# Sparse attention and a gated convolution FFN on one core: the middle batches convolved over a whole batch in one token order, query mask rows rewritten per slot, DMA planned as one first-in-first-out server

## The chip, the core and the metric

The kernel runs on one core of a Trainium2 chip. The core has five engines with an instruction stream each, taken in order: PE (TensorE, matrix products into PSUM), DVE (VectorE), ACT (ScalarE), POOL (GpSimd) and SP (SyncE, which here only issues DMA). They wait for each other through semaphores. Sixteen DMA engines move data between DRAM and the on-chip SBUF, and between places in SBUF. The metric is device time in microseconds, from the start to the end of the program.

## What is computed

```python
scores = scale * np.matmul(q, k.transpose(0, 1, 3, 2))          # 4 batches, 8 heads, 768 tokens, 64 wide
mask = (|blk_i - blk_j| <= 1) | first and last block rows and columns | 3 sampled blocks per block row
attn = softmax(np.where(mask, scores, -1e9));  x = attn @ v     # heads side by side: 768 x 512 per batch
h = np.maximum(x @ w_in, 0.0)                                   # 512 -> 1024
conv_out[t] = conv_w[0] * h[t-1] + conv_w[1] * h[t] + conv_w[2] * h[t+1]   # zeros outside the batch
gate = 1.0 / (1.0 + np.exp(-conv_out))
out = (h * gate) @ w_out                                        # 1024 -> 512
```

A block has 32 tokens, so a batch has 24. The convolution runs along the tokens and couples neighbours, so the two halves of a batch meet at a seam.

## The kernel before

*Units.* The work is cut into 8 halves (a half is 384 query tokens of one batch, `n = 2b + g`) and each half into 18 units of eight 128x128 score blocks. A unit is a set of score products on PE into one `st` buffer (line 678), one exponential of 128x1024 on ACT (line 685), and eight products with V on PE into `av` (line 705). Four pairs of heads per half take 4.5 units each. After a pair DVE takes the reciprocal of the row sums and normalises (`rcp`, `xtok`, lines 629 and 631). SP then transposes `xtok` into `xT` by DMA (line 652); the first half and the last pair go through PE instead (line 644).

*Mask.* The mask is no separate step. Q and K lie in slots with 64 rows of a head and 24 rows more (64 to 88) that hold the block mask: an indicator of the key's block on K's side, and 8000-fold penalties on Q's side. One product of 88 rows gives score plus mask. There are six slots, for the pairs P = 0 to 15 in turn, each as an ET and an OT tile (even and odd token phase). The mask rows of slot 0 are made in the start (lines 413 to 455), those of slot 1 are copied by DVE and POOL, and those of slots 2 to 5 by DMA on SP's queue (lines 444 to 463). They are the same for all pairs, since q has the same token order in every batch.

*Token order.* K is loaded with six consecutive tokens per row. Q is loaded by `src_of` (line 342) half by half: within half g, row p holds the three tokens 384g + 3p + c. The score, `xT`, `hE` and `gT` tiles of a half so have 3 column groups c of 128 rows p. A shift by one token is a shift by 128 columns, except for the outer groups, where it goes to the neighbouring row.

*Loads.* POOL issues the DMA loads that cast to 16 bits (`swdge`, line 490): q, k and v per pair, and the weights. For P = 1 to 5 (`NPE = 6`) PE transposes q and k (line 533) and DVE copies them into the slots (line 539). Later pairs go through two DMA transposes on SP (line 581) and two DVE copies from `tmp` (line 424).

*FFN.* `ffn1` (line 719) makes 8 groups of 128 channels per half: four products each into `mix` (line 729), then a scaled ReLU into `hE` by DVE (742) or ACT (740). For each pair of groups POOL copies the edge columns (`edges`, lines 829 to 835), and `conv_gate` (line 746) runs three taps of two multiplications of 384 columns each on DVE (753), two sums (759), a tanh on ACT (769), an add of one (772) and the gate (781) into `gT`. At the seam the last column of half g = 0 lacks its right neighbour; POOL saves it in `cvl` (844), and three small DVE steps and one ACT step mend it (859 to 867). `out_block` (line 784) makes three blocks of 128 tokens per half, eight products each (799), an eviction to `o2s` (422 or 424) and a store.

*Order.* Nothing of this order is in the loops. Every step is entered as an operation with a planned duration, its dependencies, buffers and a due time, and `Scheduler.run` (line 205) lists them: `forward` takes the earliest start on each engine, `backward` turns the finished plan into priorities, and this is repeated. DMA is planned as engine "DQ", with a fixed latency behind each transfer:

```python
LAT = {"PE": 0.23, "ACT": 0.20, "DVE": 0.16, "POOL": 0.20, "SP": 0.0, "DQ": 1.9}
T0, PACE0, PACE1 = 8.0, 0.91, 1
XLAT, TLAT = 3.908, 9.2201
first_u = [18 * (2 * (P // 4)) + (P % 4) * 4.5 for P in range(NP)]
load_u = [0, 0, 0, 0, 15, 19, 24, 30, 42, 50, 60, 68, 77, 86, 96, 104]
```

The plan fixes the order on every engine and, for evictions, the engine itself. The chip then runs these streams with real waits. `helpers` such as `copy_to` (lines 420 to 424) stand in the profile with one line for several tiles.

Of the kernel before, what the change touches and what calls it, by code (L numbers as in the profile page):

```python
# [24 lines left out]
class Op:  # L25
    __slots__ = ("alts", "fn", "deps", "prio", "lat", "allocs", "earliest", "pend", "outs", "ready",
                 "start", "end", "eng", "key", "uses")

    def __init__(self, alts, fn, prio, deps, lat, earliest):
        self.alts, self.fn, self.prio = alts, fn, prio  # L30
        self.deps = deps
        self.lat = lat
        self.allocs, self.uses = [], []
        self.earliest = earliest
        self.outs = []
        self.start = self.end = self.eng = None
# [12 lines left out]
FLEX = 0.0345  # L49
LAT = {"PE": 0.23, "ACT": 0.20, "DVE": 0.16, "POOL": 0.20, "SP": 0.0, "DQ": 1.9}  # L50
OWN = {"PE": 0.0, "ACT": 0.12, "DVE": 0.11, "POOL": 0.10, "SP": 0.0, "DQ": 0.0}


class Scheduler:
# [22 lines left out]
    def forward(self):  # L77
# [11 lines left out]
        while left:  # L89
# [27 lines left out]
            for e, t in free.items():  # L117
                be = None
                for o in cand:
# [5 lines left out]
                    k = (s, o.prio, o.key)  # L125
                    if be is None or k < be[0]:
                        be = (k, o, e)
                if be is not None:
                    k2 = (be[0][0], be[0][1], be[0][2], be[0][0] + be[1].alts[e])
                    if best is None or (k2[0], k2[3]) < (best[0][0], best[0][3]):  # L130
                        best = (k2, be[1], e)
            if best is None:
                raise RuntimeError("no order: buffers too few")
            k, o, e = best
            o.eng = e
            o.start = k[0]
            o.end = k[0] + o.alts[e]
# [25 lines left out]
    def backward(self, order):  # L163
# [25 lines left out]
        while ready:  # L189
# [4 lines left out]
            for j in pred[i]:  # L194
                pend[j] -= 1
                if not pend[j]:
                    ready[j] = max(0.0, max(end[m] + lat for m, lat in succ[j]))
        for o, t in zip(order, end):
            o.prio = -t
            o.outs = []  # L200
            for b in o.allocs:
                b.index = None
                b.pool.holders = []
# [10 lines left out]
def kernel(  # L214
# [11 lines left out]
    nc = tc.nc  # L226
# [10 lines left out]
    NPE = 6  # L237
    NWARM = 34

# [19 lines left out]
    NTMP, NVN, NNAT, NPT, NXK, NXT, NHE, NCV, NGT, NOS = 2, 3, 3, 5, 3, 4, 3, 3, 4, 4  # L259
# [7 lines left out]
    hE_t = many(NHE, [128, NFFC, 640], BF16, "hE")  # L267
    m_t = many(NCV, [128, 2, 768], BF16, "m")
    tn_t = many(NCV, [128, 768], BF16, "tn")
    gT_t = many(NGT, [128, NFFC, 384], BF16, "gT")  # L270
# [11 lines left out]
    bblkn = sb.tile([NB, 6, 128], BF16, tag="bblkn", name="bblkn")  # L282
# [36 lines left out]
    T0, PACE0, PACE1 = 8.0, 0.91, 1  # L319
    OFF = 32.0894  # L320
    XLAT, TLAT = 3.908, 9.2201
    S_FIRST, A_FIRST, R_FIRST, N_FIRST = 5.6663, -4, 0.1178, 0.842
    F1S, F2A, F2S = 0.03, 2.344, 0.191
    WO = 22.9467
    OFFL = 28
    PE_ = 0.0
    PASSES = 12
# [10 lines left out]

    def dma_h(dst, src):
        return lambda e: (nc.sync if e == "SP" else nc.scalar).dma_start(out=dst, in_=src() if callable(src) else src)  # L340

    def src_of(t, b, h):

        if t is q:
# [7 lines left out]
    def dst_of(t, tile_, pair):  # L352
        if t is not q:
            return tile_
        return tile_.rearrange("p h (g c) -> p (h g) c", g=2) if pair else tile_.rearrange("p (g c) -> p g c", g=2)

    hw = {}
    for x, (t, h) in enumerate([(q, 0), (k, 0), (q, 1), (k, 1)]):
        i_ = op({"SP": 0.46} if x % 2 == 0 else {"ACT": 0.42}, dma_h(dst_of(t, stage0[x], False), src_of(t, 0, h)),
                [-20, -20, -18, -19][x], lat=0.4)  # L360
        hw[x] = dq([0.9, 0.4, 0.9, 0.4][x], [i_], [-20, -19, -17, -18][x])
# [17 lines left out]
    def ind(base, sign, src):  # L379
        return lambda e: nc.gpsimd.affine_select(  # L380
            out=bblkn, in_=src, compare_op=ALU.is_ge, fill=0.0, base=base,
            pattern=[[384 * sign, 2], [sign, 3], [3 * sign, 128]], channel_multiplier=-32 * sign)
# [30 lines left out]
    def w24(e):  # L413
        w = st_t[b_w.index]
        nc.tensor.matmul(out=w[0:NB, 0:384], lhsT=aadd, rhs=bblkn[:, 0:6:2, :], start=True, stop=True)
        nc.tensor.matmul(out=w[0:NB, 512:896], lhsT=aadd, rhs=bblkn[:, 1:6:2, :], start=True, stop=True)
# [9 lines left out]

    def k_rows(t, cs, b0):

        def fn(e):
            for (u, c0, n, at) in cs:  # L430
                src = bblkn.rearrange("k (g c) (j u) -> k u c g j", g=2, u=2)[:, u, c0:c0 + 2 * n - 1:2]
                dst = t[64:88, 1, 0, at:at + n].rearrange("k c (g j) -> k c g j", g=2)
                copy_to(e, dst, src)
        return fn
    km_e = op({"ACT": 0.6, "DVE": 0.4}, k_rows(ET[0], [(0, 0, 2, 0), (1, 1, 1, 2)], 0), -15, [bn2])
    km_o = op({"ACT": 0.6, "DVE": 0.4}, k_rows(OT[0], [(0, 1, 1, 0), (1, 0, 2, 1)], 0), -14.9, [bn2])

# [6 lines left out]
    def rows_to(dst, src):  # L444
        return lambda e: nc.sync.dma_start(out=dst[64:88], in_=src[64:88])

    def dup(t):
        return lambda e: copy_to(e, t[64:88, :, 1], t[64:88, :, 0])

# [4 lines left out]
    e_mask = {0: op({"POOL": 1.0}, pool_copy(ET[0][64:88, :, 1], ET[0][64:88, :, 0]), 1.5, [qm_e, km_e])}  # L454
    o_mask = {0: op({"DVE": 0.38}, dup(OT[0]), T(1), [qm_o, km_o], earliest=T0 - 0.5)}
    for s in range(1, NSLOT):
        for t, m in ((ET, e_mask), (OT, o_mask)):
            if s == 1 and t is OT:
                m[s] = op({"POOL": 1.8}, pool_copy(t[s][64:88], t[0][64:88]), 2.5, [m[0]])
            elif s == 1:  # L460
                m[s] = op({"DVE": 0.58}, rows_by(t[s], t[0]), T(4.5 * s) - 2.5, [m[0]])
            else:
                m[s] = op({"SP": 0.46}, rows_to(t[s], t[0]), T(4.5 * s) - 6, [m[0]], lat=6.0,
                          earliest=T(18 + 2 * s) if s > 3 else 0.0)
# [4 lines left out]
    for s in range(NHE):  # L469
        def z(e, s=s):  # L470
            nc.vector.memset(hE_t[s][:, :, 639:640], 0.0)
# [14 lines left out]
    load_u = [0, 0, 0, 0, 15, 19, 24, 30, 42, 50, 60, 68, 77, 86, 96, 104]  # L486
# [3 lines left out]
    def swdge(dst, src, prio, dur, deps=(), early=0.0, alloc=None, uses=(), gate=i_sel,  # L490
              lat=None):
        i_ = op({"POOL": 0.8}, lambda e: nc.gpsimd.dma_start(out=dst(), in_=src), prio,  # L492
                list(deps) + [gate], lat=0.0, alloc=alloc, uses=uses, earliest=early)
        return i_, op({"DQ": dur}, None, prio, [i_], lat=lat or 2.4, uses=(([alloc] if alloc else []) + list(uses)))

    win_ld, wout_ld, k_iss, v_iss = [], [], {}, {}
    def qk_loads(P):
        b, h0 = P // 4, 2 * (P % 4)
        nb = Buf(P_nat)
        early, late = (T(load_u[P]), 6.0) if P > 3 else (0.0, None)  # L500
        iq, lq = swdge(lambda: dst_of(q, nat_t[nb.index][:, 0], True), src_of(q, b, slice(h0, h0 + 2)), P, 1.25,
                       early=early, alloc=nb, gate=bn1 if P == 1 else i_sel, lat=late)
        if P == 1:
            bn2.deps.append(iq)
        ik, lk = swdge(lambda: nat_t[nb.index][:, 1], src_of(k, b, slice(h0, h0 + 2)), P + 0.1 if P > 1 else 0.6, 1.1, [iq],
                   early=early + (3 if P > 3 else 0), uses=[nb], lat=late)
# [3 lines left out]
    def v_load(P, deps):  # L510
# [3 lines left out]
        v_iss[P], ld = swdge(lambda: vn_t[vb.index], src_of(v, b, slice(h0, h0 + 2)), P + 1.15 if P < 3 else P + 0.2, 1.1,  # L514
                              early=T(load_u[P]) + 6 if P > 3 else 0.0, alloc=vb, lat=6.0 if P > 3 else None,
                              gate=k_iss[max(P, min(P + 1, 3))])

# [3 lines left out]
        return op({"DVE": 0.27}, cp, T(first_u[P]) - (1 if P == 0 else 6), [ld] + deps, uses=[vb, slot_b[P]])  # L521

# [405 lines left out]
```

The softmax here doesn't subtract the row's maximum and nothing guards it: scores larger than these inputs give would overflow.

## Time and profile before

| what | value |
|---|---|
| time, median of five runs | 214.82 us (214.74 to 216.77) |
| profiled execution | 214.87 us, its span 213.2 us |
| granted TensorE clock | 1.00 |
| first, 18th and last exponential | 8.2, 27.2 and 182.8 us (end for the last two) |
| DVE convolution: taps, sums, adds of one, gates | 57.0, 34.9, 11.6, 17.9 us busy |
| ACT: exponentials, tanh | 141.8, 27.7 us busy |
| moved by DMA | 25.84 MB, 121 GB/s on average |

A "busy" time counts an instruction from its start to its end, and neighbours overlap: the next one starts before the last has ended. The sum of durations is therefore more than the time taken, and the distance between starts is the better price of one more instruction. Idle time in a row of the page is what an engine waited just before its instructions, with the releaser that came last.

### The profile page before, as it was taken

To read this page: it belongs to the slowest core of one execution; us is meant where nothing else is said; L and a number is where in the kernel's file an instruction comes from. 1 tells how busy PE (TensorE), PEld (TensorE's weight loads), DVE (VectorE), ACT (ScalarE), POOL (GpSimd) and SP (SyncE) were. 2 spreads that over 40 slices of the span, in tenths; PEclk is the share of its full clock that TensorE was granted. 3 is DMA by queue.
4 is the path that set the end of the run, shared out by engine and by line. 5 is a ranking of instruction groups with operands and counts; after the bars stand their busy time and mean duration, and the time that the engine had idled before them with its cause. 6 is when DMAs were issued, how large, how long until landed. Compare 5 with 4: busy or idle time off the path is not lost.

```text
span 213.2 us, 6588 instructions
## 1 busy us (share of the span) xinstructions
PE 198.0 (93%) x2579; PEld 150.1 (70%) x2596; DVE 190.1 (89%) x541; ACT 182.2 (85%) x227; POOL 81.2 (38%) x174
## 2 busy tenths in 40 slices
PE   7898999997999979999989979989999999998992
PEld 4687879885778857788767657767776787554441
DVE  6977439999999998399999999999999999999972
ACT  4598999999989989999979799989999999664541
POOL 8996206335524720365557201421241012343300
PEclk9999999999999999999999999999999999999999
DMA  6999997999999994999997993002100220122223
GB/s 167 149 194 205 200 202 111 120 148 151 193 119 210 145 129 71 156 149 200 171 138 115 141 189 98 18 22 68 52 23 22 92 95 22 33 84 101 100 98 148
DMA packets 50519, 25.84 MB, mean 121 GB/s; under 512 B 36320, under 2 KB 47352, under 8 KB 50488
## 3 DMA queue, kind: packets, MB, share of 16 engines
q0 software_dynamic: 18464, 11.14, 45.7%
q1 hardware_dynamic: 31592, 13.75, 32.6%
q10 hardware_dynamic: 432, 0.52, 0.8%
q8 instruction: 20, 0.33, 0.6%
q14 instruction: 11, 0.09, 0.2%
HBM read 23.08 MB, written 6.29 MB: 138 GB/s over the span
## 4 chain that ended last, share of the span: by engine, by line
DVE 50%; PE 25%; DMA 8%; ACT 7%; issue 5%; POOL 4%; ACTq 0%; POOLq 0%; DVEq 0%
DVE m L753 18%; PE st L678 9%; DVE m L759 9%; DVE hE L742 6%; ACT pt L685 6%; PE mix L799 5%; PE av L705 4%; PE mix L729 4%; DVE gT L781 4%; DVE xtok L631 4%; DMA nat<-in_k_dram 3%; DMA xT<-xtok 3%; DVE tn L772 2%; PE st L799 2%; DVE o2s L424 2%
## 5 line engine op out<-in xcount | busy, mean ns | idle before, releaser
L685 ACT ACTIVATE pt<-st 128x1024 bf16<-128x1024 f32 x144 | 141.8, 1039 | 6.9 <-PE st L678 5.5
L705 PE MATMUL av<-vt,pt 128*128 128x65 bf16 x1152 | 57.9, 193 | 0.5 <-ACT pt L685 0.2
L753 DVE TENSOR_SCALAR m<-hE,cw 128x384 bf16<-128x384 bf16 x192 | 57.0, 346 | 0.2
L705 PEld LDWEIGHTS <-pt 128*128 128x128 bf16 x1152 | 50.4, 97 | 4.8 <-ACT pt L685 0.7
L729 PE MATMUL mix<-xT,winb 128*128 128x384 bf16 x240 | 48.3, 325 | 2.6 <-DMA xT<-xtok 1.2
L829 POOL COPY hE<-hE 128x254 bf16<-128x254 bf16 x32 | 18.2, 570 | 75.5 <-DVE hE L742 51.0
L799 PE MATMUL mix<-woutb,gT 128*128 128x512 bf16 x151 | 41.0, 379 | 2.4 <-DVE gT L781 1.6
L678 PE MATMUL st<-ot 88*128 88x128 bf16 (+1 forms) x224 | 42.5, 234 | 0.3
L678 PE MATMUL st<-et,ot 88*128 88x128 bf16 (+1 forms) x224 | 42.5, 234 | 0.1
L678 PE MATMUL st<-et 88*128 88x128 bf16 (+1 forms) x208 | 40.7, 239 | 1.7 <-ACT pt L685 1.7
L678 PEld LDWEIGHTS <-ot 88*128 88x128 bf16 x448 | 34.5, 97 | 11.2 <-issue 2.0
L678 PE MATMUL st<-ot,et 88*128 88x128 bf16 (+1 forms) x208 | 40.7, 239 | 0.5 <-ACT pt L685 0.2
L678 PEld LDWEIGHTS <-et 88*128 88x128 bf16 x416 | 32.2, 97 | 9.6 <-issue 3.0
L759 DVE TENSOR_TENSOR m<-m 128x768 bf16<-128x768 bf16 x64 | 34.9, 550 | 0.1
L769 ACT ACTIVATE tn<-m 128x768 bf16<-128x768 bf16 x32 | 27.7, 865 | 5.4 <-DVE m L759 5.2
L729 PEld LDWEIGHTS <-winb 128*128 128x128 bf16 x256 | 22.1, 97 | 12.4 <-issue 1.9
L799 PEld LDWEIGHTS <-gT 128*128 128x128 bf16 x200 | 16.5, 98 | 15.5 <-DVE gT L781 3.0
L742 DVE TENSOR_SCALAR hE<-mix 128x384 bf16<-128x384 f32 x37 | 20.2, 547 | 3.9 <-PE mix L729 3.8
L781 DVE TENSOR_TENSOR gT<-tn,hE 128x768 bf16<-128x768 bf16 x32 | 17.9, 561 | 0.1
L631 DVE TENSOR_TENSOR xtok<-av,rcp 128x384 bf16<-128x384 f32 x32 | 17.6, 549 | 0.3
L492 POOL DMA_DIRECT2D vn<-in_v_dram x16 | 11.4, 716 | 12.4 <-DVE vt L519 8.7
L830 POOL COPY hE<-hE 128x254 bf16<-128x254 bf16 x32 | 15.1, 471 | 0.0
(76 smaller groups left out, 169.4 us busy)
## 6 DMA issues: line engine op xcount, KB each, us to landing
out_dram<-o2s SPq DMA_DIRECT2D x23, 256.0 KB, 2.3
vn<-in_v_dram POOLq DMA_DIRECT2D x16, 192.0 KB, 6.8
nat<-in_q_dram POOLq DMA_DIRECT2D x15, 192.0 KB, 6.3
nat<-in_k_dram POOLq DMA_DIRECT2D x15, 192.0 KB, 7.0
winb<-in_moe_w_in_dram POOLq DMA_DIRECT2D x2, 512.0 KB, 10.3
woutb<-in_moe_w_out_dram POOLq DMA_DIRECT2D x2, 512.0 KB, 9.5
xT<-xtok SPq DMA_TRANSPOSE x27, 8.8
o2s<-in_k_dram ACTq DMA_DIRECT2D x2, 192.0 KB
```

The source lines that it names most:

```text
L631: nm = op({"DVE": 0.475}, lambda e: nc.vector.tensor_tensor(out=xtok_t[xk.index].rearrange("p c h d -> p h c d"), in0=o_of()[:, :, :, 0:64 ...
L678: nc.tensor.matmul(out=st_t[stb.index][:, 128 * x:128 * (x + n_)], lhsT=QK[kc % 2][s][0:88, 1, hh, kc // 2, :], rhs=QK[par][s][0:88, 0, hh ...
L685: e_op = op({"ACT": t_act(1024)}, lambda e, stb=stb, ptb=ptb: nc.scalar.activation(out=pt_t[ptb.index], in_=st_t[stb.index], func=AF.Exp, ...
L705: nc.tensor.matmul(out=av_t[av_buf[(n, P % 4)].index][:, off:off + 65], lhsT=pt_t[ptb.index][:, 128 * x:128 * x + 128], rhs=VT[P % NSLOT][ ...
L729: nc.tensor.matmul(out=tiles[hb.index][:, 0:384], lhsT=winb[:, fc, 128 * ffc:128 * ffc + 128], rhs=xT_t[xt_buf[n].index][:, fc, :], start= ...
L742: nc.vector.tensor_scalar(out=dst, in0=src, scalar1=0.5, scalar2=0.0, op0=ALU.mult, op1=ALU.max)
L753: nc.vector.tensor_scalar(out=m_t[cb.index][:, slot, o0:o1], in0=src, scalar1=w, scalar2=None, op0=ALU.mult)
L759: nc.vector.tensor_tensor(out=m[:, 0], in0=m[:, 0], in1=m[:, 1], op=ALU.add)
L769: th = op({"ACT": 0.745}, lambda e: nc.scalar.activation(out=tn_t[cb.index], in_=m_t[cb.index][:, 0], func=AF.Tanh, bias=0.0, scale=0.5), ...
L781: nc.vector.tensor_tensor(out=o, in0=t, in1=h, op=ALU.mult)
L799: nc.tensor.matmul(out=acc()[:, 0:o1 - o0], lhsT=gT_t[gb.index][:, ffc, 128 * c:128 * c + 128], rhs=woutb[:, ffc, o0:o1], start=(ffc == 0) ...
L829: nc.gpsimd.tensor_copy(out=h[:, f0:f0 + 2, 1:128], in_=h[:, f0:f0 + 2, 384:511])
```

## The change

1. *Whole batches.* Batches 1 and 2 (those not in `NARROW = (0, 3)`) load q as k is loaded, with six consecutive tokens per row. Half g of such a batch is the token phases 3g to 3g + 2 of all rows. Its FFN1 results go into one `hE` of 6 x 128 columns, and when the second half is there `conv_gate` runs over 768 columns per channel group, with no seam. Output blocks of both halves follow after that. Batches 0 and 3 stay in halves. `hE`, `m` and `gT` become larger, with 2, 2 and 2 buffers in place of 3, 3 and 4; `tn` is gone, and its data lies in `m`.
2. *Mask rows.* Q's mask rows depend on the token order. Slots 0 to 3 begin in the narrow order, slots 4 and 5 in the wide one; when a slot passes to a batch of the other order (P = 6 to 9 and 12 to 15) `other_rows` rewrites Q's 24 rows by DMA from a kept copy. The first copies of the rows are made by DVE (one by POOL) and no longer by DMA.
3. *Heads.* `NPE` is 5: P = 5 goes through DMA transposes.
4. *Planner.* All DMAs are planned on one first-in-first-out server; loads are due 12 us ahead of their latest time; an engine may wait a little for a more urgent operation (`PATIENCE`). Due times and buffer counts are other numbers. The transposes of the last pair use `st` in place of `mix`.

```diff
-FLEX = 0.0345
+FLEX = 0
+PATIENCE = {"PE": 0.0555..., "ACT": 0.1003..., "DVE": 0.1688...}
...
-                    k = (s, o.prio, o.key)
+                    k = (o.ready, 0.0, o.key) if e == "DQ" else (max(s, t + PATIENCE.get(e, 0.0)), o.prio, o.key)
...
+            if o.ahead is not None:
+                o.earliest = span - t - o.ahead
...
-    NTMP, NVN, NNAT, NPT, NXK, NXT, NHE, NCV, NGT, NOS = 2, 3, 3, 5, 3, 4, 3, 3, 4, 4
+    NTMP, NVN, NNAT, NPT, NXK, NXT, NHE, NCV, NGT, NOS = 2, 3, 3, 5, 3, 4, 2, 2, 2, 4
...
-    XLAT, TLAT = 3.908, 9.2201
+    XLAT, TLAT = 1.3602075535012221, 1.0
...
+    def sp_dma(fn, sp, dur, prio, deps, lat, alloc=None, uses=(), by="SP"):
+        i_ = op({by: sp}, fn, prio, deps, lat=0.1, alloc=alloc, uses=uses)
+        return op({"DQ": dur}, None, prio, [i_], lat=lat, uses=list(uses) + ([alloc] if alloc else []))
...
-        if t is q:
+        if t is q and b in NARROW:
...
-                m[s] = op({"SP": 0.46}, rows_to(t[s], t[0]), T(4.5 * s) - 6, [m[0]], lat=6.0,
-                          earliest=T(18 + 2 * s) if s > 3 else 0.0)
+                m[s] = op({"DVE": 0.58}, rows_by(t[s], t[0]), T(4.5 * s) - 2.5, [m[0]])
...
+    def other_rows(P):
+        s = P % NSLOT
+        if P < NSLOT or (P // 4 in NARROW) == ((P - NSLOT) // 4 in NARROW):
+            return []
+        ops = []
+        copied = [m[x] for m in (e_mask, o_mask) for x in range(1, 4)]
+        for par, t in enumerate((ET, OT)):
+            def fn(e, par=par, t=t):
+                dst = t[s][64:88, 0].rearrange("k h c s -> k h (c s)")
+                src = t[4][64:88, 0].rearrange("k h c s -> k h (c s)")
+                if P // 4 in NARROW:
+                    src = narrow_rows[:, par].rearrange("k c s -> k (c s)").unsqueeze(1).broadcast_to([NB, 2, 384])
+                nc.sync.dma_start(out=dst, in_=src)
...
-        t0 = op({"SP": 1.3}, xp(0), due - 8, [lq], alloc=tb, uses=[nb], lat=TLAT)
+            t0 = sp_dma(xp(0), 1.25, 1.1, due - 8, [lq], TLAT, alloc=tb, uses=[nb])
...
+                for y in range(2):
+                    nc.vector.tensor_scalar(
+                        out=m_of(slot)[:, w * y:w * y + w], in0=hE_t[hb.index][:, f0 + y, 128 * x:128 * x + w],
+                        scalar1=cw[:, x, f0 + y:f0 + y + 1], scalar2=None, op0=ALU.mult)
...
+        at = 128 + (384 * g if wide else 0)
+        w = 768 if wide else 384
...
-            if ffc % 2 == 0:
+            if ffc % 2 == 0 or wide and g == 0:
                 continue
...
+            if wide:
+                todo = [(m, c, gates_n[n]) for m in (n - 1, n) for c in range(3)] if g else []
+            else:
+                todo = [(n, c, gates_n[n]) for c in range(2 + g)] + ([(n - 1, 2, [[p3o]] * 4)] if g else [])
```

## The prediction

> **What bounds the kernel now.** I read the page's busy shares first, then the chain of waits, then busy time in three stages that I cut at the 18th and the last of the 144 exponentials (27.2 us and 182.8 us in the timeline of ACT): A the start, B the middle, C the end.
>
> ```profile
> PE 198.0 (93%) x2579; PEld 150.1 (70%) x2596; DVE 190.1 (89%) x541; ACT 182.2 (85%) x227; POOL 81.2 (38%) x174
> DVE  6977439999999998399999999999999999999972
> DVE 50%; PE 25%; DMA 8%; ACT 7%; issue 5%; POOL 4%; ACTq 0%; POOLq 0%; DVEq 0%
> L753 DVE TENSOR_SCALAR m<-hE,cw 128x384 bf16<-128x384 bf16 x192 | 57.0, 346 | 0.2
> ```
>
> ```profile
> 0.00:27.20 27.20, 24.07 (x344) 20.00 (x344) 19.29 (x60) 20.66 (x26) 19.42 (x32) 1.00 1.15 183
> 27.20:182.80 155.60, 148.66 (x2100) 117.55 (x2115) 146.07 (x410) 147.57 (x178) 54.24 (x124) 1.00 0.85 115
> 182.80:213.20 30.40, 25.22 (x137) 12.50 (x137) 24.70 (x72) 14.02 (x26) 7.53 (x18) 1.00 0.25 96
> ```
>
> In the stage rows the columns are PE, PEld, DVE, ACT, POOL, clock, DMA, GB/s. DVE holds half of the chain and its row of tenths is 9 from 35 us on but for one dip at 80 us. Yet PE and ACT stand at 149 and 148 of B's 155.6 us: three engines are nearly full at once, so a cut on one is worth only what the next allows. A mean duration overlaps its neighbours, so I cost with the distance from one start to the next, read from the timeline:
>
> ```profile
> 77.33 0.53 DVE L753 TENSOR_SCALAR m<-hE,cw 128x384 bf16<-128x384 bf16 x2
> 77.79 0.34 DVE L772 TENSOR_SCALAR tn<-tn 128x768 bf16<-128x768 bf16 x1
> 78.06 0.54 DVE L759 TENSOR_TENSOR m<-m 128x768 bf16<-128x768 bf16 x1
> 78.53 0.54 DVE L781 TENSOR_TENSOR gT<-tn,hE 128x768 bf16<-128x768 bf16 x1
> 79.00 0.18 DVE L629 RECIPROCAL rcp<-av 128x6 f32<-128x6 f32 x1
> ...
> 78.63 0.84 ACT L769 ACTIVATE tn<-m 128x768 bf16<-128x768 bf16 x1 [0.28 <-DVE m L759]
> 79.38 1.92 ACT L685 ACTIVATE pt<-st 128x1024 bf16<-128x1024 f32 x2
> 81.19 0.21 ACT L864 ACTIVATE tp<-cvp 128x8 bf16<-128x8 f32 x1
> ```
>
> Steps: a tap of 384 columns 0.23 us, the add of one 0.27, a sum or a gate of 768 columns 0.47, a tanh 0.75, an exponential 0.91. On PE the same timeline gives 0.44 for a unit's scores, 0.25 for its eight AV products, 0.64 for one FFN1 group of four, 0.216 for one product of 512 columns (0.43 for two).
>
> **The change part by part.**
>
> *Whole-batch convolution.* Batches 1 and 2 run 8 gates of 1536 columns in place of 16 of 768. The listing of the built program's instructions (an order, with no times in it) gives the counts. Taps: 192 at 0.23 become 96 at 0.23 and 48 of 768 columns. No such tap is in the trace; it lies between the 768-column add of one (0.27) and two taps of 384 (0.46). From 384 columns at 0.23 and a cost of 0.1 us for 384 more (the 0.23 less a fixed 0.13; the add of one carries no scalar from memory and is 0.06 cheaper), I take 0.33: 44.2 to 37.9, a gain of 6.3 (ends 0 at 0.46 and 9.2 at 0.27). Sums: 64 x 0.47 become 32 x 0.47 and 16 of 1536 columns at 0.87 (twice the streaming, one fixed part of 0.07): gain 1.1. Adds of one and gates by the same reasoning: 0.5 and 0.6. The seam column (L859 to L867) goes for two batches: 6 small instructions, 0.7. DVE gains 9.2 in all. ACT: 32 tanh x 0.75 become 16 x 0.75 and 8 of 1536; exponential and tanh differ by 0.16 for 256 columns, so 1536 cost 0.75 + 0.5 = 1.25: gain 2.0. POOL loses 16 edge copies, 8 seam copies and 8 saves of cvl; POOL waits 75 us for DVE, so nothing.
>
> [...]
>
> *Mask rows.* Eight copies of 72 KB on SP's queue (L445, 0.71 us each, six between 7.7 and 12.3 us) become DVE copies: seven of 1536 columns where there was one, three of 768 for one, four of 384. From the 64x1536 copies of tmp (start to start 0.47 to 0.59) seven are 3.9; with the small ones 5.9 for 1.2 before, so 4.7 more on DVE, nearly all in A. A's DVE row is busy 19.3 of 27.2, so it fits if its order is right. The row for the one mask copy of before is dearer, 0.86 us, while POOL was copying ot. [...] At 0.86 each the seven are 6.0, an increase of 6.8, which no longer fits A; but POOL has one such copy of 1.48 us, so I use 0.55. In return 432 KB leave a stage that moves 198 GB/s: 2.2 us of transfer ahead of the key load that ends the chain's longest start wait (issued 11.17, landed 18.57). Sixteen rewrites of 36 KB are added to SP's queue when slots change order (P 6 to 9, 12 to 15); each waits for its slot there, with the xT transposes queued behind it. In the listing each stands beside the norm of the same head pair, about when the slot has been free for long, so I count 0 (at most 16 x 0.7 = 11 us of SP time, which is idle over half).
>
> *Heads.* P5 moves from PE to DMA transposes: PE 12 x 0.055 less, DVE four copies of 0.52 less and two of 0.55 more, SP two issues of 1.2 more. In DVE's listing the copy et<-tmp of P5 stands ahead of the first FFN1 eviction of half 0. Its key load now queues behind P4's loads and both w_in halves: at 1 us per load (198 GB/s) about 28 us, plus two issues and 5.6 us landing (the shortest of tmp): 34 to 35 us. DVE can reach it at about 30. Behind it stand evictions that PE's third FFN1 group needs at about 33 us. So 0 to 4 us on DVE, 0 to 2.5 on the path; I take 1.
>
> *Buffers and planner.* hE, m and gT fall from 3, 3, 4 half-batch buffers to 2, 2, 2, tn is folded into m, so a tanh on ACT can hold DVE up one gate sooner; the listing places other DVE work between. I take 0, at most 24 gates x 0.1 = 2.4. The loads of middle q read 1536 bytes in a row in place of 768; no row separates that: 0 to a microsecond.
>
> *The sum by stage,* counts of the listing times the steps:
>
> | work, us | A | B | C |
> |---|---|---|---|
> | DVE | 18.2 to 24.8 | 139.4 to 126.7 | 20.1 to 21.5 |
> | PE | 19.8 to 21.3 | 146.6 to 142.3 | 24.0 to 26.6 |
> | ACT | 18.7 to 19.4 | 146.0 to 141.3 | 14.0 to 16.7 |
>
> PE's total does not change (190.4 to 190.2): nothing but its idle can be won. In B that is 155.6 - 146.6 = 9.0. DVE leaves with 12.7 less (gates 10.8 and seams 0.7 by the wide form and by one gate put off to C, heads 4.2 to A; tmp 1.1, FFN1 evictions 1.9 and a mask 0.6 more; output evictions 0.6 less), and PE and ACT become the bound with 4.3 and 4.7 less. With PE's idle unchanged B ends 4.3 sooner, with all of it gone 13. In the dip at 80 us, where DVE had room, two stages of nine units ran at PE's own pace (10.06 and 10.19 us for 10.05 and 10.06 of work), so some idle does go: I take 3.0 of the 9.0, B 7.3 shorter. C holds one more half-batch gate and 1.5 more output blocks: DVE +1.4, PE +2.6 with 2.9 of PE idle ahead of the last stores; I take +1.7. A: DVE's added work against earlier keys, +0.5 (-1 to +3). P5: +1. Sum: -7.3 + 1.7 + 0.5 + 1.0 = -4.1. The profiled execution took 214.87 (span 213.2), the median of five 214.82, so they agree: **210.8 us**.
>
> **Rivals.** *The end takes it back* (chance 0.23). B gains only the 4.3 with unchanged idle, C costs PE's whole 2.6, A and P5 1.5: 214.7. For it: full PE and ACT, and 26.6 us of PE work after the last exponential. Against: the stage at 80 us.
>
> *Transposed tokens land late; slower* (0.20). PE runs in order, so FFN1 stalls until xT has landed:
>
> ```profile
> xT<-xtok SPq DMA_TRANSPOSE x27, 8.8
> ...
> 116.76 6.98 DMA xT<-xtok
> 123.74 0.04 issue
> 123.78 0.32 PE mix L729
> ```
>
> Before, half 4 had six units between its attention's end and FFN1 and stalled 1.2 us. After, halves 1, 4, 5, 6 have 7, 8, 4 and 5 units (before 8.5, 6, 7, 8). The last pair of half 4 took 3.9 us from the last exponential to its issue (112.9 to 116.8) and 7 to land. At that sum, 10.9, halves 5 and 6 with 4.6 and 5.7 us of room (1.15 us a unit) wait 6.3 and 5.2: 11.5 less the 4.1 is 222 at worst; half of it gives 216.5. Past 128 us, where the loads had ended, landing took 2.3 us; with DVE no longer behind, 2.5 to issue is likely (AV 1.5, norm 0.7), and 4.8 leaves 0.2. From a sum of 7.2 us on (waits of 2.6 and 1.5) the gain is gone. The last loads now go out later, so it is open.
>
> *DVE alone was the bound* (0.15): B loses 10 to 11, the rest as above: 207.
>
> *Wide taps don't gain* (within the first rival): at 0.46 for 768 columns DVE in B still falls by 6.4, more than PE's 4.3.
>
> **How the numbers follow.** The forecast has 0.42, DVE alone 0.15, the end 0.23, late landing 0.20. The range 206.5 to 216.5 spans the forecast's own 208 to 212.5, the better case and most of the rest. About 1% (2.1 us) is what a measurement of this kernel can tell from no change. Faster by over 1% (under 212.7): the forecast and the good case, 0.57. Within: 0.24. Slower (over 217): 0.19, mostly late landing.
>
> **What would show it.** Taps of 768 columns near 0.33 from start to start; DVE's work in B down by some 12 us and gaps in its row of tenths; the last exponential at 175 to 178 us in place of 182.8; then 31 to 32 us to the end. Wrong if PE waits for xT by more than 3 us in all, if DVE stalls on et<-tmp near 30 us for more than 4, or if the middle ends no sooner.

## The result, and the profile after

The changed kernel takes 213.1 us (median of 20 runs, 212.44 to 214.97); the kernel before, run beside it, takes 215.19 us. The ratio is 0.9915 with a 95% interval of 0.9897 to 0.9934: 1.8 us faster (the medians differ by 2.1), clear of noise, where 4.1 had been forecast. The profiled execution took 213.17 us, its span is 211.5 us. Ratios count only executions at the chip's usual pace, and since the profiled execution of late_p5 below ran at a lower clock (0.992), its stages are read from its repetition late_p5b.

The lines of the page that answer to those of before:

```profile
PE 199.1 (94%) x2576; PEld 150.4 (71%) x2590; DVE 186.8 (88%) x465; ACT 182.9 (86%) x218; POOL 71.1 (34%) x150
DVE  7899990999689999983899999997999999999952
DVE 49%; PE 24%; DMA 14%; issue 9%; POOL 2%; SPq 1%; DVEq 0%; POOLq 0%
DVE m L811 17%; DVE m L817 8%; PE mix L853 7%; DMA tmp<-nat 6%; DVE hE L794 6%; PE st L730 5%; DMA nat<-in_q_dram 5%; DVE xtok L678 4%; DVE gT L830 4%; PE mix L781 3%; DMA xT<-xtok 3%; PE av L757 2%; PE av L386 2%; DVE m L828 2%; PE st L853
```

DVE's busy time has fallen by 3.2 us only: it lost 10.8 us in B, but gained 6.3 in A, where eight more mask copies (4.6 us) and four more head copies (2.2 us) now stand, and 1.3 in C. New is a 0 in DVE's row of tenths (the seventh slice, 32 to 37 us), and the chain of waits now holds 14% of DMA where it held 8%, most of it in `tmp<-nat` and the q load: a wait for a transposed key or query has come onto the path.

Busy time of the whole kernel by stage, cut again at the 18th and the 144th exponential (columns as in the prediction: PE, PEld, DVE, ACT, POOL, clock, DMA, GB/s). The cuts lie within 0.03 us of the ends of these exponentials, 28.42 and 178.83 us:

```profile
0.00:28.45 28.45, 25.67 (x362) 21.42 (x363) 25.59 (x72) 22.71 (x28) 20.51 (x34) 1.00 1.13 173
28.45:178.82 150.37, 145.20 (x2064) 114.95 (x2076) 135.33 (x319) 143.46 (x161) 42.86 (x93) 1.00 0.79 119
178.82:211.50 32.68, 28.18 (x151) 13.98 (x151) 25.93 (x76) 16.70 (x31) 7.72 (x23) 1.00 0.28 105
```

| stage, us | before | after | measured | forecast |
|---|---|---|---|---|
| A, to the 18th exponential | 27.21 | 28.45 | +1.24 | +0.5 |
| B, 18th to 144th | 155.67 | 150.37 | -5.30 | -7.3, and +1.0 for P5: -6.3 |
| C, to the end | 30.32 | 32.68 | +2.36 | +1.7 |
| span | 213.2 | 211.5 | -1.7 | -4.1 |

All terms have the sign that was forecast, and all three came out on the dear side, by 0.74, 1.0 and 0.66 us. Together these are the 2.4 us that are missing. The experiments look for the cause of each.

### The profile page after: what moved, and what is told of

Same layout as the page of the kernel before. It is cut to its first block, busy times and chain, and to the rows that moved or that the text cites. A ratio compares the mean times of both kernels' runs of the same rounds, so it can differ in the third digit from the quotient of the medians.

```text
span 211.5 us, 6504 instructions
## 1 busy us (share of the span) xinstructions
PE 199.1 (94%) x2576; PEld 150.4 (71%) x2590; DVE 186.8 (88%) x465; ACT 182.9 (86%) x218; POOL 71.1 (34%) x150
## 4 chain that ended last, share of the span: by engine, by line
DVE 49%; PE 24%; DMA 14%; issue 9%; POOL 2%; SPq 1%; DVEq 0%; POOLq 0%
DVE m L811 17%; DVE m L817 8%; PE mix L853 7%; DMA tmp<-nat 6%; DVE hE L794 6%; PE st L730 5%; DMA nat<-in_q_dram 5%; DVE xtok L678 4%; DVE gT L830 4%; PE mix L781 3%; DMA xT<-xtok 3%; PE av L757 2%; PE av L386 2%; DVE m L828 2%; PE st L853 2%
## 5 line engine op out<-in xcount | busy, mean ns | idle before, releaser
L757 PE MATMUL av<-vt,pt 128*128 128x65 bf16 x1152 | 56.9, 193 | 1.6 <-DVE xtok L678 1.3
L781 PE MATMUL mix<-xT,winb 128*128 128x384 bf16 x240 | 48.8, 325 | 2.7 <-DMA xT<-xtok 1.7
L811 DVE TENSOR_SCALAR m<-hE,cw 128x384 bf16<-128x384 bf16 (+1 forms) x144 | 47.5, 380 | 0.5 <-POOL hE L892 0.3
L889 POOL COPY hE<-hE 128x254 bf16<-128x254 bf16 x24 | 13.2, 552 | 88.7 <-DVE hE L794 63.8
L817 DVE TENSOR_TENSOR m<-m 128x768 bf16<-128x768 bf16 (+1 forms) x48 | 32.7, 692 | 0.5
L853 PEld LDWEIGHTS <-gT 128*128 128x128 bf16 x200 | 17.8, 98 | 15.9 <-issue 2.1
L826 ACT ACTIVATE m<-m 128x768 bf16<-128x768 bf16 (+1 forms) x24 | 25.8, 1074 | 3.7 <-DVE m L817 3.7
L794 DVE TENSOR_SCALAR hE<-mix 128x384 bf16<-128x384 f32 x40 | 21.9, 549 | 4.9 <-PE mix L781 4.7
L830 DVE TENSOR_TENSOR gT<-m,hE 128x768 bf16<-128x768 bf16 (+1 forms) x24 | 17.0, 710 | 0.3
L890 POOL COPY hE<-hE 128x254 bf16<-128x254 bf16 x24 | 14.0, 583 | 0.0
```

What stands on the lines that cost most here:

```text
L757: nc.tensor.matmul(out=av_t[av_buf[(n, P % 4)].index][:, off:off + 65], lhsT=pt_t[ptb.index][:, 128 * x:128 * x + 128], rhs=VT[P % NSLOT][ ...
L781: nc.tensor.matmul(out=tiles[hb.index][:, 0:384], lhsT=winb[:, fc, 128 * ffc:128 * ffc + 128], rhs=xT_t[xt_buf[n].index][:, fc, :], start= ...
L794: nc.vector.tensor_scalar(out=dst, in0=src, scalar1=0.5, scalar2=0.0, op0=ALU.mult, op1=ALU.max)
L811: nc.vector.tensor_scalar(out=m_of(slot)[:, w * y:w * y + w], in0=hE_t[hb.index][:, f0 + y, 128 * x:128 * x + w], scalar1=cw[:, x, f0 + y: ...
L817: nc.vector.tensor_tensor(out=m_of(0), in0=m_of(0), in1=m_of(1), op=ALU.add)
L826: th = op({"ACT": t_act(2 * w) + 0.055}, lambda e: nc.scalar.activation(out=m_of(1), in_=m_of(0), func=AF.Tanh, bias=0.0, scale=0.5), due ...
```

## The experiments

Ratios are to the kernel before, which ran beside each; 0.001 is 0.215 us, and a difference against after is the difference of two such ratios. Times of single exponentials come from one trace of each version. Five versions that leave B's program as it is (after, start_order and the three cuts in the end) spent 149.6 to 150.4 us in B, 150.0 in the mean, so a difference of half a microsecond there says nothing. Moves of single steps are made after planning: a step gets a new place, the rest keeps its order.

### The wait for P5's transpose

In the timeline of DVE after (start, duration, in brackets the idle time before), the copy of P5's transposed rows stands ahead of everything that follows:

```profile
31.30 0.36 DVE L540 COPY vt<-vn 128x768 bf16<-128x768 bf16 x1
36.79 0.55 DVE L443 COPY et<-tmp 64x1536 bf16<-64x1536 bf16 x1 [5.13 <-DMA tmp<-nat]
37.27 0.54 DVE L794 TENSOR_SCALAR hE<-mix 128x384 bf16<-128x384 f32 x1
37.73 0.18 DVE L676 RECIPROCAL rcp<-av 128x6 f32<-128x6 f32 x1
37.94 0.56 DVE L678 TENSOR_TENSOR xtok<-av,rcp 128x384 bf16<-128x384 f32 x1
38.53 0.55 DVE L443 COPY ot<-tmp 64x1536 bf16<-64x1536 bf16 x1
```

The eviction, the reciprocal and the norm behind it were held for the whole wait. late_p5 puts the two copies behind two evictions, a norm and four taps, and after them in the order the issue of P7's two transposes, which need the buffer of `tmp` that these copies free; late_p5b is the same kernel again.

```diff
+            if P == 5:
+                moved += [(ce, 36.65), (co, 36.66)]
+            if P == 7:
+                moved += [(t0.deps[0], 36.67), (t1.deps[0], 36.68)]
```

> The changed kernel with the two copies of P5 out of tmp moved behind what stood next on DVE (two FFN1 evictions, a normalisation, four taps). Theory (the copy of P5 waited 5.1 us for its DMA transpose with evictions behind it, and this costs the path about 1 us as predicted, perhaps 2): the wait of 5.1 us goes or falls under 1 us, the last exponential comes 1 to 2 us sooner than 178.8, total 1 to 2 us less than the changed kernel. Rival (DVE has slack there, the wait is free): the wait goes, the total stays within 0.5 us.

> The same kernel as late_p5, run for a second timing and for a trace in which every stage can be read. Theory (the wait of VectorE for P5's transpose held up the FFN1 evictions and the norm behind it, for 2.5 us, and nothing later gives it back): 210.2 to 211.0 us, ratio to before 0.976 to 0.982, and the 54th exponential ends 2 to 3 us sooner than after's 68.4 with the stretch from there to the end as in after (143.1 us). Rival (the gain was a lucky order of two instructions further on, and is given back): the 54th no more than 1 us sooner, or the stretch behind it over 144.5 us.

late_p5 took 210.68 us, ratio 0.9795 [0.9773, 0.9816]; late_p5b 211.16 us, 0.9813 [0.9775, 0.985]: 2.2 to 2.6 us less than after. The same stretch of DVE in late_p5b:

```profile
31.28 0.36 DVE L541 COPY vt<-vn 128x768 bf16<-128x768 bf16 x1
34.08 0.56 DVE L799 TENSOR_SCALAR hE<-mix 128x384 bf16<-128x384 f32 x1 [2.43 <-PE mix L786]
34.64 0.20 DVE L681 RECIPROCAL rcp<-av 128x6 f32<-128x6 f32 x1
34.87 0.56 DVE L683 TENSOR_TENSOR xtok<-av,rcp 128x384 bf16<-128x384 f32 x1
...
37.88 0.75 DVE L444 COPY et<-tmp 64x1536 bf16<-64x1536 bf16 x1
38.65 0.73 DVE L444 COPY ot<-tmp 64x1536 bf16<-64x1536 bf16 x1
```

The first eviction runs 3.2 us sooner, and nobody waits for the copies. The norm of that head pair is sooner as well, by 3.1 us. DVE carries the delay on: in after a norm further down starts at 52.39 us (50.52 in late_p5b), its xT is issued at 52.98 (51.10), and PE waits for that xT. The chain of waits in after (start, duration), then PE's timeline:

```profile
52.39 0.56 DVE xtok L678
...
52.98 5.40 DMA xT<-xtok
...
58.42 0.32 PE L781 MATMUL mix<-xT,winb 128*128 128x384 bf16 x1 [1.72 <-DMA xT<-xtok]
```

late_p5b has no such wait. P7's transposes, which were moved too, are issued at nearly the same time in both (39.89 and 39.56 us), so the gain is that of the two copies. The exponentials show both parts: from the 31st to the 46th those of late_p5b end 0.7 us sooner, from the 48th to the 67th 2.4 to 2.6. So the smaller part of the cost comes from the evictions held at 36.8 us, and the larger from the xT that was late at 58.4. The 54th exponential ends at 65.85 us, not 68.38. Of these 2.5 us 0.7 are given back by the 72nd (11.41 us from the 63rd, 10.67 in after), and 1.9 last to the 144th. A part is given back, but the theory holds: one wait, priced at 1 us, cost about 2.

### What the whole-batch gates are worth

all_narrow keeps the change but gates all four batches per half (one small copy each for the ET and OT tiles is added, so that slots 4 and 5 begin in the narrow order too).

```diff
-    NARROW = (0, 3)
+    NARROW = (0, 1, 2, 3)
```

> The changed kernel with no whole batch: all four batches in halves as before, no rewrites of mask rows, the new planner, buffers, start and heads kept. Theory (the gain of the change is DVE's 9 us by the wide gates, of which the middle keeps some 5): 4 to 6 us slower than the changed kernel, slower than before as well, since the later start and the wait for P5 stay. Rival (the gain comes from the planner, the wide gates bring little because PE and ACT are the bound): within 1.5 us of the changed kernel.

It took 217.96 us, ratio 1.0108 [1.0062, 1.0155]: 4.1 us more than after, and slower than before. The planner worked out a new order for it, and it has the changed kernel's 2, 2 and 2 buffers where before had 3, 3 and 4, so this is the price of the old gates in the new surroundings, with fewer buffers; the two were not tried apart. The stages say where it lies: A and B end almost as in after (144th exponential at 178.31 us), and the end takes 38.1 us in place of 32.7. One more gate stands behind the last exponential (10 for 9), with 12 more taps and 4 more sums. A stage alone doesn't tell what a gate is worth; the sum of the stages does.

### Which engine bounds the middle

Three kernels cut the work of one engine in B, and a fourth makes all three cuts.

```diff
# less_dve_mid: 16 taps of 768 columns, 8 sums of 1536
-                for y in range(2):
+                for y in range(2 if w == 384 or x else 0):
...
-        ad1 = op({"DVE": t_d2(2 * w)}, add,
+        ad1 = op({"DVE": t_d2(2 * w)}, lambda e: w == 768 or add(e),
# less_act_mid: 8 tanh of 1536
-        th = op({"ACT": t_act(2 * w) + 0.055}, lambda e: nc.scalar.activation(
+        th = op({"ACT": t_act(2 * w) + 0.055}, lambda e: w == 768 or nc.scalar.activation(
# less_pe_mid: 24 output products of batch 1
+                    if n in (2, 3) and a in (1, 2):
+                        return
```

> In the gates of 1536 columns the tap of the left neighbour and the first sum are left out: 16 taps and 8 sums, about 12.7 us of DVE between 60 and 180 us; the order of everything else stays. Theory (after the change DVE is no longer the bound of the middle, PE and ACT are): under 3 us less in total. Rival (DVE is still the bound of the middle): 8 us or more less.

> The eight tanh of 1536 columns are left out: 8 x 1.25 = 10 us of ACT in the middle. Theory (PE and ACT together are the bound of the middle): 2 to 6 us less. If ACT alone were the bound, 8 to 10; if DVE or PE alone, under 1.

> Of each of the six output blocks of batch 1, all in the middle, four of the eight products are left out: 24 products, 5.2 us of PE. Theory (PE and ACT together are the bound): 1 to 3.5 us less. If PE alone were the bound, 4.5 to 5; if DVE or ACT alone, under 0.7.

> The three cuts of less_dve_mid, less_act_mid and less_pe_mid in one kernel: left out are 16 taps with 8 sums (12.7 us of VectorE), the eight tanh of 1536 columns (10 us of ScalarE) and 24 output products of batch 1 (5.2 us of TensorE). Theory (the engines take turns as the bound, piece by piece, so that one engine's cut is met by the next engine at once): with all three eased the longest engine's work summed over the pieces of nine exponentials falls from 151.4 to 142.9 us, so the time falls by 5 to 9 us against after, to 204 to 208, far over the 2.1 to 2.7 us that the three cuts gave singly. Rival (no engine bounds the middle: waits, latencies and due times between the engines do): the cuts only add up, 2 to 3 us, 210 to 211.

| kernel | time, us | ratio | B, us |
|---|---|---|---|
| after | 213.1 | 0.9915 [0.9897, 0.9934] | 150.4 |
| less_dve_mid | 212.03 | 0.9856 [0.9804, 0.9907] | 149.6 |
| less_act_mid | 212.87 | 0.9888 [0.984, 0.9936] | 150.0 |
| less_pe_mid | 212.65 | 0.9875 [0.9819, 0.9931] | 149.7 |
| cut_all | 208.89 | 0.974 [0.9683, 0.9798] | 146.5 |

Each cut of 5 to 13 us on one engine gave at most 1.3 us, for ACT and PE less than had been expected, and each interval overlaps that of after. All three together gave 3.8 us. By the times alone that could still be the sum of the three gains (2.7 us); B tells more: the single cuts took 0.8 us off its mean of 150.0 between them, all three together took 3.5. So the cuts don't simply add up: the engines take turns as the bound, and each is next in line behind the other. Where ACT had the turn it shows in single pieces: from the 90th to the 99th exponential after took 12.26 us, less_act_mid 10.95; but the nine behind it took 9.64 in after and 10.96 there, so another wait took back what ACT had given.

The 5 to 9 us forecast for cut_all were too many. They rest on a fall of 8.5 us in the longest engine's work, summed over B's 14 pieces of nine exponentials. In the traces the busy time of the busiest engine of each piece sums to 154.8 of B's 155.7 us in before, 147.2 of 150.4 in after, 147.1 to 147.9 with one cut, and 143.7 of 146.5 in cut_all: 3.5 less than after, about what B gave. In cut_all PE is busy for 141.6 us of B, ACT for 133.6 and DVE for 124.0, so PE is what is left. That an engine is busy does not show that it was the bound, so this sum fits the reading and does not prove it.

### Which engine bounds the end

less_end_pe leaves out 24 output products of batch 2 (5.2 us of PE), less_dve_end the third tap and second sum of the last half's four gates (3.6 us of DVE), less_end_both does both. All of it stands behind the last exponential.

```diff
# less_end_pe
+                    if n in (4, 5) and a in (1, 2):
+                        return
# less_dve_end
+        last = gb is gt_buf.get(3) and o == 384
-        m2 = op({"DVE": tm}, mul(2, 1),
+        m2 = op({"DVE": tm}, lambda e: last or mul(2, 1)(e),
-        ad2 = op({"DVE": t_d2(2 * w)}, add,
+        ad2 = op({"DVE": t_d2(2 * w)}, lambda e: last or add(e),
```

> Of each of the six output blocks of batch 2, all of which run after the last exponential, four of the eight products are left out: 24 products, 5.2 us of PE; the order stays. Theory (the end is bound by PE since the whole-batch convolution has put output blocks off): 4 to 5 us less. Rival (the end is bound by DVE's gates of batch 3, as before): 0 to 1 us less.

> After, with the third tap and the second sum of the four gates of the last half left out (8 taps of 384 columns and 4 sums of 768, about 3.6 us of VectorE, all behind the last exponential). Theory (the end is bound by VectorE's gates of the last half, which is why 5.2 us less of TensorE there gave 0.5): the end from the 144th exponential falls from 32.7 us by 2 to 3.6, and the time by as much, to 209.5 to 211. Rival (VectorE and TensorE bound the end by turns, as in the middle): under 1.2 us, 212 or more.

> The cuts of less_end_pe and less_dve_end together: 24 output products of batch 2 (5.2 us of TensorE) and the third tap and second sum of the last half's four gates (3.6 us of VectorE) are left out. Theory (VectorE's gates and TensorE's stock of output products bound the end by turns, each taking over when the other is eased): the end from the 144th exponential falls from 32.7 us to 29 to 31, and the time by 2 us or more against after, to 209 to 211 us. Rival (a chain of single waits bounds it: gate, tanh, gate, product, eviction, store): the end keeps 32 us or more and the time is 212 or more.

| kernel | time, us | ratio | C, us |
|---|---|---|---|
| after | 213.1 | 0.9915 [0.9897, 0.9934] | 32.7 |
| less_end_pe | 212.53 | 0.9894 [0.987, 0.9918] | 32.6 |
| less_dve_end | 212.2 | 0.9875 [0.9831, 0.9919] | 32.3 |
| less_end_both | 209.9 | 0.977 [0.9743, 0.9797] | 29.9 |

Alone the cuts gave 0.0 and 0.4 us of C, together 2.8, and by the times less_end_both alone is clear of after. The same five microseconds of the end, in the windows of after, of less_end_pe and of less_dve_end (one fence each; the first column behind the length is PE, the third DVE), show how:

```profile
195.00:200.00 5.00, 4.95 (x24) 2.25 (x23) 4.96 (x19) 1.91 (x3) 0.00 (x0) 1.00 0.39 150
```

```profile
195.00:200.00 5.00, 3.80 (x16) 1.40 (x16) 4.97 (x19) 1.88 (x4) 0.00 (x0) 1.00 0.31 119
```

```profile
195.00:200.00 5.00, 5.00 (x25) 2.25 (x23) 3.15 (x12) 2.42 (x6) 0.00 (x0) 1.00 0.30 115
```

In after both engines are full. Ease PE, and DVE stays full; ease DVE, and PE stays full. Both work off a stock: DVE the gates of batch 3, PE the six output blocks of batch 2. The end needs both.

### The start

In after the first exponential came 0.94 us later than before (9.09 for 8.15 us). Four kernels tried to bring it forward. start_order lets DVE take the sampled-block row between its two casts; both adds late_p5 to it; late_start, on late_p5, also moves the row's products ahead of the transposes on PE, and two of ACT's copies behind exponentials. late_mask, on late_p5, leaves the casts in front and moves only DVE's copy of the key mask and ACT's narrow row.

```diff
# start_order
+            moved += [(casts[1], 4.40), (a4, 4.41), (casts[0], 4.42), (km_e, 4.43)]
# late_start: in addition, of the even parity and the narrow row
+            moved += [(wmm, 5.24), (qn, 9.14)]
+    moved.append((narrow_op[0], 12.3))
# late_mask
+            moved += [(km_e, 6.95)]
+    moved.append((narrow_op[0], 12.3))
```

> The changed kernel with DVE's first steps in the order of before: one cast, the sampled-block row, then the second cast and the copy of the key mask rows. Theory (the first exponential came 0.9 us later because the mask row was put behind a mask copy and two casts): first exponential at 8.3 to 8.6 in place of 9.1, and 0.5 to 0.7 us less in total, since 18 exponentials follow at a pace that nothing catches up. Rival (the later wait near 30 us swallows it): first exponential sooner, total unchanged.

> Both moves together. Theory: the two gains add, 1.7 to 2.5 us less than the changed kernel (about 210.8 to 211.3 on the scale where before is 215.0). Rival: less than the larger of the two alone, since the end is set by something else.

> late_p5, and the start changed on three engines: VectorE takes the sampled-block row between its two first casts, TensorE takes the six mask-row products ahead of the first transposes, and ScalarE copies the middle batches' mask row behind the first exponential and the narrow row behind the fifth. Theory (in start_order the row was ready 0.7 us sooner but its products stood behind the transposes on TensorE, and two copies stand ahead of the first exponential on ScalarE): first exponential at 8.1 to 8.4 us instead of 9.1, the 18th ends 0.6 to 1.0 us sooner, and the time is 0.6 to 1.0 us under late_p5b, ratio about 0.975. Rival (the q load's landing sets the first exponential, or the stretch from the 1st to the 18th is bound by VectorE's 18 us of work there and takes the gain back): first exponential at 8.8 or later, or the 18th at the same time as in late_p5b, and no gain.

> late_p5, and of the start only two steps moved: on VectorE the copy of the key's mask rows stands behind the first head's two copies and no longer ahead of the casts, and on ScalarE the narrow row stands behind the fifth exponential. Theory (these two hold the first exponential): sampled-block row ready at 5.8 instead of 6.16, first exponential at 8.2 to 8.5 us instead of 9.1, the 18th ends 0.5 us sooner or more, and the time is 0.4 to 0.9 us under late_p5's, ratio 0.976 to 0.979. Rival (VectorE's 18 us of work before the 9th exponential, with the mask rows of the other slots, sets the 18th whatever the first does): first exponential sooner, but the 18th ends at 28.3 to 28.5 as in every version of the change, and the time is that of late_p5.

| kernel | time, us | ratio | first exponential starts | 18th ends |
|---|---|---|---|---|
| after | 213.1 | 0.9915 [0.9897, 0.9934] | 9.09 | 28.42 |
| start_order | 213.47 | 0.9932 [0.9899, 0.9964] | 9.19 | 28.51 |
| both | 211.55 | 0.9852 [0.9813, 0.9892] | 9.36 | 28.68 |
| late_start | 212.04 | 0.9846 [0.9797, 0.9895] | 9.23 | 28.36 |
| late_mask | 210.73 | 0.9801 [0.9775, 0.9827] | 8.68 | 28.19 |

The first three missed. With the second cast behind the row, the first transposes on PE came 0.6 us later or more (5.77 and 6.49 us for 5.15), and with them the head copies that the first scores need: the row was early and the heads were late. late_mask brought the first exponential 0.41 us sooner and the 18th 0.23, less than expected, and the time stayed that of late_p5. Something else filled the stretch to the 18th. The windows of 18 to 28.5 us, of before and of after (third column DVE), say which engine:

```profile
18.00:28.50 10.50, 9.39 (x168) 8.47 (x169) 5.60 (x14) 9.71 (x11) 3.63 (x5) 1.00 1.34 202
```

```profile
18.00:28.50 10.50, 9.58 (x183) 9.05 (x181) 10.08 (x26) 9.55 (x11) 5.13 (x8) 1.00 1.22 187
```

DVE has next to no room left in this stretch. And one of its copies was far dearer than its like (timelines of DVE and POOL after):

```profile
8.93 0.55 DVE L443 COPY et<-et 24x1536 bf16<-24x1536 bf16 x1
9.98 1.70 DVE L443 COPY et<-et 24x1536 bf16<-24x1536 bf16 x1
...
9.78 1.48 POOL L459 COPY ot<-ot 24x1536 bf16<-24x1536 bf16 x1
```

The second copy began 0.2 us after POOL's and ended 0.42 us after it: it looks as if it stood still until POOL's was done. Before holds the same meeting with another offset (timelines of DVE and POOL): there the copy began when POOL's was 70% done, and ended 0.41 us after it.

```profile
9.34 0.86 DVE L424 COPY et<-et 24x1536 bf16<-24x1536 bf16 x1
...
8.31 1.48 POOL L453 COPY ot<-ot 24x1536 bf16<-24x1536 bf16 x1
```

apart is late_mask with this copy of slot 2 put behind the six copies that followed it.

```diff
+                if s == 2 and t is ET:
+                    moved.append((m[s], 12.6))
```

> late_mask, and VectorE's mask copy for slot 2 (24x1536, which took 1.70 us at 9.98 beside GpSimd's copy of 1.48) stands four copies later, at about 12.5 us, when GpSimd's copy has ended. Theory (the two copies contend, and the 1.15 us over the usual 0.55 are lost on a VectorE that is full to the 18th exponential): the copy takes 0.55 to 0.6, the copies that take its place beside GpSimd's lose less than 0.4 between them, the 18th exponential ends 0.4 to 1.1 us sooner than late_mask's 28.1, and the time is 0.4 to 1.0 us under late_mask's, ratio 0.975 to 0.978. Rival (whatever VectorE does beside GpSimd's copy is slowed as much, or the exponentials of this stretch wait for TensorE and not for these copies): the 18th at 27.9 or later and the time as late_mask's, ratio 0.979 to 0.982.

The timelines of apart at the same place:

```profile
9.96 0.55 DVE L586 COPY et<-mix 64x768 bf16<-64x768 bf16 x1
10.54 0.56 DVE L586 COPY ot<-mix 64x768 bf16<-64x768 bf16 x1
...
13.17 0.58 DVE L444 COPY et<-et 24x1536 bf16<-24x1536 bf16 x1
...
9.65 1.48 POOL L460 COPY ot<-ot 24x1536 bf16<-24x1536 bf16 x1
```

The moved copy takes 0.58 us, and the head copies that stand beside POOL's now, with their input in PSUM, take their usual 0.55. The 18th exponential ends at 27.18 us, 1.0 sooner than in late_mask, and the 144th is 1.3 sooner (175.24 for 176.53). The first, which starts before the old place of the moved copy, already comes 0.23 us sooner, so 0.8 us of the 1.0 are the move's. The span is 207.7 us for 209.2. The time is 210.16 us, ratio 0.9774 [0.9742, 0.9807]. Against late_mask's ratio the intervals overlap, so by time alone the gain isn't shown; in the traces each exponential from the 5th on is 0.67 to 1.3 us sooner. apart has the lowest ratio of the versions that compute the whole output, 4.9 us under before and 3.0 under after, and late_p5 alone holds most of it.

## Why the prediction was wrong in size

Of the 2.4 us that are missing, 0.9 are P5's wait, 0.7 the start, 0.7 the end and 0.1 the middle.

- *Direction, and the mechanism of the middle.* Both hold. DVE's busy time in B fell by 10.8 us, PE's by 3.5, ACT's by 4.2, and B by 5.3 only, because PE and ACT stood next in line. The reading "three engines are nearly full at once" is what the cuts show.
- *B, -7.3.* The term holds once P5's wait is taken out of it: late_p5b's B is 148.5 us, 7.2 less than before. That is in part luck, since two misses cancel: PE's busy time fell by 3.2 where 4.3 had been counted, and PE's idle (length less busy) went from 6.9 to 3.0, 3.9 where 3.0 had been taken. The step of a wide tap came as forecast, 0.33 us, as these lines of after give (0.66 for two, then the next start); a tanh of 1536 steps 1.37 for 1.25:

```profile
122.58 0.74 DVE L811 TENSOR_SCALAR m<-hE,cw 128x768 bf16<-128x768 bf16 x2
123.24 0.68 DVE L443 COPY o2s<-mix 128x512 f32<-128x512 f32 x1
...
113.72 1.50 ACT L826 ACTIVATE m<-m 128x1536 bf16<-128x1536 bf16 x1
115.09 3.80 ACT L737 ACTIVATE pt<-st 128x1024 bf16<-128x1024 f32 x4
```

  No row of before shows the fixed 0.13 of a tap, whose one width there is 384 columns, nor the 0.07 of a sum; they were the author's estimates. After's 0.33 for 768 columns and 0.23 for 384 give 0.13, and its sums step by 0.47 for 768 columns and 0.87 for 1536, which gives 0.07. The usual step is not the mean: over the 48 wide taps that is 0.39, as it was 0.27 for the 192 narrow ones of before with their usual 0.23.
- *P5, "0 to 4 us on DVE, 0 to 2.5 on the path; I take 1".* This step failed, in size and in its path. The load landed when forecast, at 27.94 us for "about 28"; the second transpose, issued at 29.40, then took 7.30 us where 5.6 had been taken, so the landing came at 36.70 and not at 34 to 35 (chain of after):

```profile
17.33 10.61 DMA nat<-in_q_dram
...
28.02 1.33 SPq L626
...
29.40 7.30 DMA tmp<-nat
```

  DVE waited 5.13 us, over the 4 that had been named as a sign of being wrong, and about 2 of them were on the path (1.9 at the 144th exponential, 2.2 to 2.6 by the times). The prediction priced the wait by the evictions behind it. They cost 0.7 us; the larger part came some 20 us later, through a norm and its xT, for which PE waited 1.72 us. That path was thought of only as a rival of its own, with another cause.
- *A, +0.5.* It came to 1.24. "At 0.86 each the seven ... no longer fits A; but POOL has one such copy of 1.48 us, so I use 0.55": this step failed, in an unforeseen way. Five of the seven took 0.55 and one 0.83; the seventh met POOL's copy and took 1.70. Moving it away brought the 18th exponential 0.8 us sooner, the larger part of what A had lost; moving the two steps of late_mask brought 0.2. The two head copies that stood beside the same POOL copy in apart, with their input in PSUM, took 0.55 and 0.56 us; why the mask copy was held and they were not, no trace shows. The price of 0.86 in before fits the tail of the same wait: that copy too ended 0.41 us after POOL's. Spread over seven copies it was the wrong sum, left out it was wrong too.
- *C, +1.7.* It came to 2.36. "2.9 of PE idle ahead of the last stores" was to absorb 0.9 of PE's 2.6. PE's busy time there rose by 3.0 (25.1 to 28.2 us), and its idle gave 0.7: PE waits there on DVE, which got 1.3 us more to do (24.6 to 25.9 busy), and the end needs both engines, as less_end_both shows.
- *The mask rows written by DMA, 0.* The trace shows no cost: on SP's queue their line waits for the scores of the old order for 3.1 us in all, 0.8 at the longest (total, times, longest):

```profile
SPq L558 <- PE st L730: 3.1, 5, 0.8
```

  A version without them and otherwise the same was not tried.
- *Rivals.* xT landing late: PE waited 1.7 us for it in all, 1.2 before, so the sign of 3 us did not come; but the 1.7 are the larger part of what P5's wait cost. The end taking the gain back came nearest: 214.7 was forecast, with B's gain 4.3; the end took 2.36 of B's 5.3. DVE alone as the bound of before is refuted by B, which lost 7.2 us without P5's wait for DVE's 10.8; after it is not DVE either, since less_dve_mid gives 1.3 us for 12.7. That wide taps don't gain is refuted by their step.

## What to carry to other kernels

Where three engines are nearly full (94 to 96% of B in before), a cut on one is worth what the next leaves (here at most 1.3 us for 5 to 13), so cut several, and expect no more than what the busiest engine of each short piece loses; here even that was forecast at over twice what came. Then look for the single waits: here a copy that waits for a DMA ahead of ready work on an engine that takes its work in order, and one copy that met another engine's copy, cost 3 us together and were had back by giving a handful of instructions another place. Follow such a wait past the work right behind it: most of its cost can show up later (here some 20 us), where something that it delayed is needed. When a step is moved to an engine that is said to have room, look at that engine over the stretch it must fit, and at what GpSimd copies in those microseconds.

## What the runs showed of the hardware

- A mask copy on DVE, SBUF to SBUF, 24x1536 of bf16, usually took 0.55 us. Begun beside a GpSimd copy of the same form of 1.48 us it took 1.70 (after) and 0.86 (before); in both it ended 0.4 us after GpSimd's, which fits waiting and not sharing. Two copies from PSUM to SBUF on DVE beside the same GpSimd copy took 0.55 and 0.56 (apart).
- The wide taps took longer beside GpSimd's copies too. In after the 33 that began beside no copy and no load issue of GpSimd took 0.37 to 0.42 us, the nine that began beside one of its edge copies 0.54 to 0.60.
- Steps on DVE, from start to start: a tap of 384 and of 768 columns usually 0.23 and 0.33 us (after), an add of one of 768 columns 0.27 (before) and of 1536 columns 0.47 (after). Both grow by 0.10 for 384 columns, so an estimate of the part that each instruction pays once is 0.13 for a tap, which reads its factor from SBUF, and 0.07 for the add of a constant.
- Beside GpSimd's issue of a load it was mixed in after: 0.40 to 0.65 us for six wide taps, 0.83 for one mask copy and 0.55 for others. What decides it stays open.
- P5's q load in after, issued at 17.33 us behind a head pair's loads and both halves of w_in (14.25 to 17.37), took 10.6 us to land, where the median of its kind is 6.1.
